# Three v buffers, an earlier unit 4, w1 in halves and earlier conversions in an attention and expert kernel on one core

## The chip, the cores and the metric

The kernel runs on one core of a Trainium2 chip. The metric is the device time of one execution in microseconds (us). A change of about 2% is what can be told from no change with this kernel. "Profile" means one execution recorded by the hardware profiler; its span is the part in which the core works, and the execution's own time is a little longer.

## The reference

```python
# q, k, v: (8 batches, 8 heads, 576, 64), fp32
scores = (q @ k.T) / sqrt(64)            # masked: 0 <= row - column < 64
attn = softmax(scores)
x = (attn @ v), heads side by side       # (8, 576, 512)
pooled = x.mean(axis=1)                  # (8, 512)
logits = pooled @ w_gate                 # (8, 8 experts)
e = argmax(logits); g = max(softmax(logits))
out[b] = g[b] * (relu(x[b] @ w1[e[b]]) @ w2[e[b]])   # w1: 512x1024, w2: 1024x512
```

Which expert's weights a batch needs is known only when its whole attention output has been pooled, so the load of w1 and w2 of a batch waits for its gate.

## The kernel before

The work is cut into 16 units `u`, each four heads of one batch; units 2b and 2b+1 are batch b. For a unit, q and k come in by `load_qk` as two tiles `qn` and `kn` (the transfer turns fp32 into bf16), TensorE transposes them (`transpose_qk`), and `leave_qk` copies them out of PSUM: q on ScalarE (ACT), k on VectorE (DVE) unless told otherwise. `scores(u, c)` makes a third of the banded scores and their exponentials; from unit 2 on DVE multiplies them with a mask. `values(u, s)` multiplies with v and `norm` divides by the row sums into `x`. `transpose_x` turns x round and sums it for the gate.

v of a batch is loaded once by `load_v(b)`: a memset of one element on GpSimd (POOL) claims the buffer `vn`, then SyncE (SP) issues the transfer. `cast_part` turns half a batch, one unit, into two fp16 copies: "whole" makes `va`, and "low" and "high" make `vb`, the same rows shifted by 64. `cast_v` does all three on DVE.

`gate(b)` ends with a register load on GpSimd; `load_w1` and `load_w2` then issue the weights (fp32 to fp16) from GpSimd's queue. Batch 0's w1 comes in four column quarters. An expert is eight `expert_up` and five `expert_down` chunks; `experts(amount)` emits the next chunks between the pieces of attention, so the experts of batch b run beside the attention of later units. Output rows leave through six `ob` buffers, copied by DVE and issued by SyncE. `busy(n)` emits n matmuls that nothing uses.

The order of everything on each engine is the order in which it is written: first a prelude that ends with units 0 to 3 and the first gate, then a loop over steps t = 4 to 19, in which unit t's attention, the preparation of unit t+1 and the expert chunks alternate. In even steps `next_gate` runs the gate of batch t/2 - 1 and issues its weights. GpSimd issues q, k and weights on one queue (q0 in the profile), SyncE v and the output on another (q1).

Of the kernel before, what the change touches and what calls it, by code (L numbers as in the profile page):

```python
# [156 lines left out]
def kernel(  # L157
# [22 lines left out]
    def P(ins):  # L180
        tc.keep_in_program_order(ins)
        return ins

    const = ctx.enter_context(tc.tile_pool(name="const", bufs=1))
    qkn = ctx.enter_context(tc.tile_pool(name="qkn", bufs=6))
    vpool = ctx.enter_context(tc.tile_pool(name="vpool", bufs=2))
    qkt = ctx.enter_context(tc.tile_pool(name="qkt", bufs=2))
    ptp = ctx.enter_context(tc.tile_pool(name="ptp", bufs=6))
    xpool = ctx.enter_context(tc.tile_pool(name="xpool", bufs=2))
# [18 lines left out]
    def load_qk(u):  # L208
        qn = qkn.tile([128, 2, NT * D], BF16, tag="qn")
        kn = qkn.tile([128, 2, NT * D], BF16, tag="kn")  # L210
        P(nc.gpsimd.dma_start(out=qn, in_=qv[u]))
        P(nc.gpsimd.dma_start(out=kn, in_=kv[u]))
        qk_tiles[u] = (qn, kn)

    v_tiles = {}

    def load_v(b):
        vn = vpool.tile([128, NM, D], FP32, tag="vn")

        P(nc.gpsimd.memset(vn[:, 0, 0:1], 0.0))  # L220
        P(nc.sync.dma_start(out=vn, in_=vv[b]))
        v_tiles[b] = vn

# [13 lines left out]
    load_qk(0)  # L237
    ident = const.tile([128, 128], BF16)
    make_identity(nc, ident)
    load_v(0)  # L240
    load_qk(1)
    identh = const.tile([128, 128], FP16)
    P(nc.vector.tensor_copy(out=identh, in_=ident))
# [220 lines left out]
    w2q = moe_w2.rearrange("e (g p i) d -> e p g i d", p=128, i=2)  # L464

    gparts = {}

# [46 lines left out]

    experts_of = {}

    NQ = 4

    def w1_parts():
        return weights[0][0].rearrange("p k f -> p (k f)").rearrange(  # L520
            "p (h k f) -> p h k f", h=NQ, k=KB)

# [10 lines left out]
                in_=w1e[experts_of[b]].squeeze(0)))  # L533

    def load_w2(b):
        i = FB // NQ if b == 0 else 4
        P(nc.gpsimd.dma_start(
            out=weights[b][1].rearrange("p (g i) d -> p g i d", i=i),
            in_=(w2q if b == 0 else w2e)[experts_of[b]].squeeze(0)))

    h_tiles = {}

    def expert_up(b, ft):
        if b == 0:
            w1t, cols = w1_parts()[:, ft // 2], slice(ft % 2, 256, 2)
        else:
            w1t, cols = weights[b][0], slice(512 * (ft // 4) + ft % 4, 512 * (ft // 4 + 1), 4)
        xT = xt_tiles[b]
        if ft == 0:
            h_tiles[b] = hpool.tile([128, FB, S], FP16, tag="hT", name=f"hT{b}")  # L550
        hT = h_tiles[b]
        php = psum.tile([128, 2, 512], FP32, tag="ps")
        for kb in range(KB):
            for sc in range(2):
                P(nc.tensor.matmul(  # L555
                    out=php[:, sc, 0:288], lhsT=w1t[:, kb, cols],
                    rhs=xT[:, kb, ts(sc, 288)],
                    start=(kb == 0), stop=(kb == KB - 1)))
# [79 lines left out]
    def busy(n):  # L638

        sp = psum.tile([128, 2, 512], FP32, tag="ps", name="idle")  # L640
        for _ in range(n):
            P(nc.tensor.matmul(out=sp[:, 0, :], lhsT=spin[:, 0:128], rhs=spin,
                               start=True, stop=True))
# [33 lines left out]
    add_outside(0, 1)  # L677
    add_outside(0, 2)

    after = const.tile([128, 1], BF16)  # L680
    P(nc.gpsimd.tensor_copy(out=after, in_=kt_tiles[0][:, 0:1]))
    load_qk(2)
    load_qk(3)
    load_v(1)
    for c in range(3):
        scores(0, c)
    make_masks()
    transpose_qk(1, 0)
    transpose_qk(1, 1)
    cast_v(0)  # L690
    cast_part(1, "high", nc.gpsimd)
    cast_part(1, "low", nc.gpsimd)
    cast_part(1, "whole")
    for c in range(3):
        add_outside(1, c)
    for c in range(3):
        scores(1, c)
    busy(2)
    values(0, 0)
    values(0, 1)  # L700
    transpose_qk(2, 0)
    values(1, 0)
    values(1, 1)
    transpose_qk(2, 1, leave=False)
    leave_qk(2, 1, A)
    busy(2)
    pool_mm(0)
    busy(3)
    pool_mm(1)
    pool_parts()  # L710
    busy(2)
    gate(0, False)
    load_w1(0)
    cast_v(2)
    load_qk(4)
    load_v(2)
    load_w2(0)
    load_qk(5)
    load_qk(6)
    for c in range(3):  # L720
        scores(2, c)
        if c == 0:
            gate_weight(0)
    transpose_x(0, eng=A, parts=False)
    transpose_x(1, eng=V, parts=False)
    transpose_qk(3, 0)
    transpose_qk(3, 1)
    cast_v(3)
    busy(4)
    for c in range(3):  # L730
        scores(3, c)

# [12 lines left out]
    transpose_qk(4, 1)  # L745
    experts(1.0)
    transpose_x(3)
    load_v(3)

    for t in range(START + 1, NU + LAG):  # L750
        pace = per_step / 8.0 * 0.96
        on, prev, ahead = t < NU, START + 1 < t <= NU, t + 1 < NU

        def next_gate():
            b = t // 2 - 1
            gate(b)
            load_w1(b)
            if START + 1 < t < NU - 4:
                load_qk(t + 4)
            load_w2(b)  # L760
            if t == START + 1:
                load_qk(7)

        if t % 2 == 1 and (t + 3) // 2 < B:
            load_v((t + 3) // 2)
        for u in [8, 9] if t == 5 else [t + 4] if t % 2 == 1 else []:
            if u < NU:
                load_qk(u)
        if prev:
            transpose_x(t - 1)  # L770
        if t == NU:
            okc = row_check()
        if on:
            scores(t, 0)
        experts(pace)
        if t == START + 1:
            next_gate()
            cast_v(4)
        if on:
            scores(t, 1)  # L780
        experts(pace)
        if START + 1 < t <= NU and t % 2 == 0:
            next_gate()
        if on:
            scores(t, 2)
        experts(pace)
        if ahead:
            transpose_qk(t + 1, 0)
            cast_part(t + 1, "whole")
        experts(pace)  # L790
        if on:
            values(t, 0)
        if ahead:
            cast_part(t + 1, "low")
        experts(pace)
        if ahead:
# [48 lines left out]
```

## Time and profile before

| what | value |
|---|---|
| median of 3 runs | 237.91 us (236.73 to 240.49) |
| profiled execution | 237.41 us, span 235.7 us, mean granted clock 0.973 |
| PE / DVE / ACT / POOL busy | 207.7 / 142.3 / 121.5 / 42.8 us |
| first gate's w1 issued, first expert matmul | 28.71, 33.43 us |
| q0 / q1 moved | 26.22 / 18.88 MB |

PE is TensorE, PEld its weight loads. A row of the timeline gives the start and length in us, engine, line and operation, the tiles written and read, the number of instructions, and in brackets how long the engine sat idle before it and what ended that. A row of the chain gives start, length and what the end of the program hung on then. In the tables by stretch the clock that TensorE was granted and the share of the 16 DMA engines stand behind the engines; that share is a sum over overlapping packets and can pass 1.

### The profile page before, as it was taken

How to read it: one execution, taken by the hardware profiler on the slowest of the kernel's cores; microseconds unless marked ns; L12 is line 12 of the kernel's file. 1: busy time of each engine (PE TensorE's matmuls, PEld its weight loads, DVE VectorE, ACT ScalarE, POOL GpSimd, SP SyncE). 2: the span in 40 equal slices, each digit the busy share in tenths (PEclk: the TensorE clock that was granted, in tenths of full speed). 3: DMA queues.
4: the chain of work that ended last, by engine and by line, in shares of the span. 5: the costliest groups of instructions: out<-in, count | busy, mean ns of one | idle time of the engine just before them, and what ended most of it. 6: DMA issues, size and time to landing. Idle time of an engine off the chain costs nothing.

```text
span 235.7 us, 7000 instructions
## 1 busy us (share of the span) xinstructions
PE 207.7 (88%) x3020; PEld 141.4 (60%) x3020; DVE 142.3 (60%) x315; ACT 121.5 (52%) x205; POOL 42.8 (18%) x72
## 2 busy tenths in 40 slices
PE   7657879979799978999899989999999999998980
PEld 2427557725478545875578556865687558647640
DVE  2559597539856594838764697559675964531140
ACT  2461576933376606693467617680758265605500
POOL 7252192041300160007000330020001100200000
PEclk9995899979999999999999999999999999999997
DMA  5999299999999999997999999999960995199342
GB/s 76 221 216 256 47 116 220 236 243 246 228 247 265 246 243 250 230 247 152 228 244 235 198 180 261 229 253 173 246 177 3 161 233 169 11 197 237 116 145 66
DMA packets 31222, 45.64 MB, mean 194 GB/s; under 512 B 2512, under 2 KB 22992, under 8 KB 31184
## 3 DMA queue, kind: packets, MB, share of 16 engines
q0 software_dynamic: 15152, 26.22, 63.2%
q1 hardware_dynamic: 15232, 18.88, 26.7%
q8 instruction: 25, 0.41, 0.7%
q10 hardware_dynamic: 800, 0.03, 0.2%
q14 instruction: 13, 0.11, 0.1%
HBM read 61.90 MB, written 9.44 MB: 303 GB/s over the span
## 4 chain that ended last, share of the span: by engine, by line
PE 46%; DMA 24%; ACT 11%; DVE 11%; issue 3%; POOL 1%; POOLq 1%; SPq 0%
PE php L555 23%; DMA w1t<-in_moe_w_dram 19%; PE pso L569 9%; DMA vn<-in_v_dram 5%; PE tp L329 5%; PE op L408 4%; ACT xT L453 4%; ACT pt L384 4%; ACT hT L559 3%; DVE vb L298 2%; DVE dst L298 2%; DVE pt L386 2%; PE tp L445 2%; DVE ob L572 1%; PE sp L369 1%
## 5 line engine op out<-in xcount | busy, mean ns | idle before, releaser
L555 PE MATMUL php<-xT,w1t 128*128 128x288 f16 x512 | 71.5, 288 | 5.3 <-DMA w1t<-in_moe_w_dram 4.7
L559 ACT ACTIVATE hT<-php,gatew 128x576 f16<-128x576 f32 x64 | 47.4, 746 | 33.3 <-PE php L555 33.3
L569 PE MATMUL pso<-w2t,hT 128*128 128x512 f16 x256 | 61.6, 386 | 2.6 <-DMA w2t<-in_moe_w_dram 1.8
L555 PEld LDWEIGHTS <-w1t 128*128 128x128 f16 x512 | 53.6, 113 | 13.3 <-DMA w1t<-in_moe_w_dram 5.6
L384 ACT ACTIVATE pt<-sp 128x768 f16<-128x768 f32 x48 | 37.7, 813 | 13.8 <-PE sp L369 13.8
L569 PEld LDWEIGHTS <-hT 128*128 128x128 f16 x256 | 23.4, 99 | 29.2 <-issue 3.0
L453 ACT ACTIVATE xT<-tp 128x576 f16<-128x576 f16 x28 | 17.9, 646 | 33.5 <-PE tp L445 33.5
L572 DVE COPY ob<-pso 128x512 f32<-128x512 f32 x32 | 21.9, 685 | 19.9 <-PE pso L569 19.6
L386 DVE TENSOR_TENSOR pt<-pt,masks 128x768 f16<-128x768 f16 x42 | 23.1, 557 | 17.3 <-ACT pt L384 16.8
L531 POOL DMA_DIRECT2D w1t<-in_moe_w_dram x7 | 5.0, 717 | 139.0 <-DVE gatew L513 75.1
L424 DVE TENSOR_TENSOR x<-op,linv 128x640 f16<-128x640 f32 x32 | 26.4, 824 | 1.1
L342 ACT COPY dst<-tp 128x1152 bf16<-128x1152 bf16 x16 | 18.0, 1124 | 12.1 <-PE tp L329 12.1
L298 DVE COPY dst<-tp 128x1152 bf16<-128x1152 bf16 x15 | 20.3, 1350 | 4.3 <-PE tp L329 4.0
L408 PE MATMUL op<-vb,pt 128*64 128x65 f16 x320 | 17.7, 202 | 4.1 <-DVE vb L298 3.5
L408 PEld LDWEIGHTS <-pt 128*64 128x64 f16 x640 | 14.4, 116 | 10.7 <-issue 6.0
L408 PE MATMUL op<-va,pt 128*64 128x65 f16 x320 | 17.4, 202 | 0.0
L369 PE MATMUL sp<-dst 64*64 64x128 bf16 (+1 forms) x672 | 15.4, 214 | 1.9 <-DVE dst L298 1.9
L298 DVE CAST va<-vn 128x1152 f16<-128x1152 f32 x16 | 12.7, 796 | 5.9 <-DMA vn<-in_v_dram 5.8
L298 DVE COPY vb<-va 64x1152 f16<-64x1152 f16 (+1 forms) x30 | 15.8, 527 | 0.6
L369 PEld LDWEIGHTS <-dst 64*64 64x64 bf16 x672 | 10.4, 106 | 8.9 <-issue 4.4
L476 DVE SCALAR_TENSOR_TENSOR gpart<-wg,pooled,gpart 128x8 f32<-128x8 f32 x21 | 4.8, 226 | 17.9 <-ACT xT L453 17.9
L445 PE MATMUL tp<-identh,x 128*128 128x128 f16 x160 | 11.6, 220 | 3.3 <-DVE x L424 2.5
(69 smaller groups left out, 166.6 us busy)
## 6 DMA issues: line engine op xcount, KB each, us to landing
w2t<-in_moe_w_dram POOLq DMA_DIRECT2D x8, 1024.0 KB, 17.5
out_dram<-ob SPq DMA_DIRECT2D x32, 256.0 KB, 8.6
w1t<-in_moe_w_dram POOLq DMA_DIRECT2D x7, 1024.0 KB, 10.2
qn<-in_q_dram POOLq DMA_DIRECT2D x16, 288.0 KB, 15.3
kn<-in_k_dram POOLq DMA_DIRECT2D x16, 288.0 KB, 16.5
w1t<-in_moe_w_dram POOLq DMA_DIRECT2D x4, 256.0 KB, 6.1
out_dram<-ob SPq DMA_DIRECT2D x16, 64.0 KB, 6.5
vn<-in_v_dram SPq DMA_DIRECT2D x8, 0.2 KB, 18.1
```

The costliest lines, as they stand in the source:

```text
L298: P(eng.tensor_copy(out=out, in_=in_))
L342: P(nc.scalar.copy(out=dst.rearrange("p (x r t) -> p x r t", x=2, t=NT), in_=view))
L369: P(nc.tensor.matmul(out=sp[64 * half:64 * half + 64, s, 64 * (qblk - 6 * c):64 * (qblk - 6 * c) + n], lhsT=kT[64 * s:64 * s + 64, ts(kblk ...
L384: P(nc.scalar.activation(out=pt, in_=sp[:, :, 0:384], func=AF.Exp, scale=scale))
L386: P(nc.vector.tensor_tensor(out=pt, in0=pt, in1=masks[:, c].rearrange("p s g w -> p s (g w)"), op=ALU.mult))
L408: P(nc.tensor.matmul(out=op[64 * half:64 * half + 64, xx, 65 * jj:65 * jj + 65], lhsT=pt[:, s, 64 * (g % 6):64 * (g % 6) + 64], rhs=win, s ...
L424: P(nc.vector.tensor_tensor(out=x[:, :, h0 * D:(h0 + 2) * D].rearrange("p j (x c) -> p x j c", x=2), in0=view[:, :, :, 0:64], in1=li[:, :, ...
L453: P(nc.scalar.activation(out=xT[:, kb, :], in_=tp[:, kl, 0:S], func=AF.Copy, accum_out=pooled[:, b, kb:kb + 1]))
L555: P(nc.tensor.matmul(out=php[:, sc, 0:288], lhsT=w1t[:, kb, cols], rhs=xT[:, kb, ts(sc, 288)], start=(kb == 0), stop=(kb == KB - 1)))
L559: P(nc.scalar.activation(out=hT[:, ft].rearrange("p (sc s) -> p sc s", sc=2), in_=php[:, :, 0:288], func=AF.Relu, scale=gatew[:, b:b + 1]))
L569: P(nc.tensor.matmul(out=pso[:, 0, :], lhsT=hT[:, fb, ts(mt, 128)], rhs=w2t[:, fb, :], start=(fb == 0), stop=(fb == FB - 1)))
L572: P(nc.vector.tensor_copy(out=ob, in_=pso[:, 0, :]))
```

## The change

Prelude: v of batch 0 is issued between q and k of unit 0; v of batch 1 is claimed by a copy from k of unit 0; GpSimd converts vb of unit 0 and DVE does all of unit 1, where GpSimd had unit 1; units 3 and 4 are loaded behind these conversions, unit 4 thus ahead of the first gate; w1 of batch 0 comes in halves, w2 right behind it in the layout of the other batches; v of batch 2 is claimed by a copy from the first half of w1; four `busy` calls are shorter or gone; k of unit 3 leaves on ScalarE; units 2 and 3 are converted later. Loop: `load_v` moves from the head of odd steps into `next_gate`, for a batch that is two steps further on, into a third buffer; conversions of unit t+1 stand in the first half of step t from t = 6 on.

```diff
-    vpool = ctx.enter_context(tc.tile_pool(name="vpool", bufs=2))
+    vpool = ctx.enter_context(tc.tile_pool(name="vpool", bufs=3))
...
         P(nc.gpsimd.dma_start(out=qn, in_=qv[u]))
+        if u == 0:
+            load_v(0)
         P(nc.gpsimd.dma_start(out=kn, in_=kv[u]))
...
-    def load_v(b):
+    def load_v(b, behind=None):
         vn = vpool.tile([128, NM, D], FP32, tag="vn")
-        P(nc.gpsimd.memset(vn[:, 0, 0:1], 0.0))
+        if behind is None:
+            P(nc.gpsimd.memset(vn[:, 0, 0:1], 0.0))
+        else:
+            P(nc.gpsimd.tensor_copy(out=vn[:, 0, 0:1], in_=behind))
...
-    NQ = 4
+    NQ = 2
...
-    after = const.tile([128, 1], BF16)
-    P(nc.gpsimd.tensor_copy(out=after, in_=kt_tiles[0][:, 0:1]))
+    load_v(1, kt_tiles[0][:, 0:1])
     load_qk(2)
-    load_qk(3)
-    load_v(1)
...
-    cast_v(0)
-    cast_part(1, "high", nc.gpsimd)
-    cast_part(1, "low", nc.gpsimd)
-    cast_part(1, "whole")
+    cast_part(0, "high", nc.gpsimd)
+    cast_part(0, "low", nc.gpsimd)
+    load_qk(3)
+    load_qk(4)
+    cast_part(0, "whole")
+    cast_v(1)
...
-    busy(2)
     values(0, 0)
     values(0, 1)
     transpose_qk(2, 0)
+    busy(1)
     values(1, 0)
     values(1, 1)
+    pool_mm(0)
     transpose_qk(2, 1, leave=False)
     leave_qk(2, 1, A)
-    busy(2)
-    pool_mm(0)
-    busy(3)
+    busy(1)
     pool_mm(1)
     pool_parts()
-    busy(2)
     gate(0, False)
     load_w1(0)
-    cast_v(2)
-    load_qk(4)
-    load_v(2)
     load_w2(0)
     load_qk(5)
+    load_v(2, w1_parts()[:, 0, 0, 0:1])
     load_qk(6)
+    load_v(3)
...
-    transpose_qk(3, 1)
+    transpose_qk(3, 1, leave=False)
+    leave_qk(3, 1, A)
+    cast_v(2)
     cast_v(3)
-    busy(4)
+    busy(3)
...
             load_w2(b)
+            if t // 2 + 2 < B:
+                load_v(t // 2 + 2)
...
-        if t % 2 == 1 and (t + 3) // 2 < B:
-            load_v((t + 3) // 2)
...
+        if ahead and t > 5:
+            cast_part(t + 1, "whole")
         if on:
             scores(t, 0)
...
             next_gate()
-            cast_v(4)
+        if ahead and t > 5:
+            cast_part(t + 1, "low")
         if on:
             scores(t, 1)
...
+        if ahead and t > 5:
+            cast_part(t + 1, "high")
...
         if on:
             scores(t, 2)
+        if t == START + 1:
+            cast_v(t)
         experts(pace)
         if ahead:
             transpose_qk(t + 1, 0)
-            cast_part(t + 1, "whole")
...
-        if ahead:
-            cast_part(t + 1, "low")
...
         if on:
             values(t, 1)
-        if ahead:
-            cast_part(t + 1, "high")
+        if t in (4, 5):
+            cast_v(t + 1)
```

Lines from 205 on have other numbers in the changed kernel (the copy of line 298 is 303 there, the transfer of v in line 221 is 227).

First place: GpSimd from the first v to the first gate. `vn` is v as loaded, `vb_122` a shifted fp16 copy, `eidx` the expert's number. Before:

```order
L212 DMA kn<-in_k_dram 128x2x576
L211 DMA qn<-in_q_dram 128x2x576
L212 DMA kn<-in_k_dram 128x2x576
L220 MEMSET vn 128x1
L298 COPY vb_122<-vn 64x18x64 x2
L501 TENSOR_LOAD eidx
L528 ISA
L528 DMA w1t_579<-in_moe_w_dram 128x4x256
```

And in the changed kernel:

```order
L226 COPY vn<-dst 128x1
L211 DMA qn<-in_q_dram 128x2x576
L214 DMA kn<-in_k_dram 128x2x576
L303 COPY vb_122<-vn 64x17x64
L303 COPY vb_122<-vn 64x18x64
L211 DMA qn<-in_q_dram 128x2x576
L214 DMA kn<-in_k_dram 128x2x576
L211 DMA qn<-in_q_dram 128x2x576
L214 DMA kn<-in_k_dram 128x2x576
L505 TENSOR_LOAD eidx
L532 ISA
L532 DMA w1t_572<-in_moe_w_dram 128x4x512
```

Two more units of q and k stand between the conversions and the gate; the claim of the second v went ahead of unit 2.

Second place: SyncE's queue, v (`vn`) against the writes of the output (`out_dram`). Before:

```order
L221 DMA vn<-in_v_dram 128x36x64 x4
L573 DMA out_dram<-ob 128x512 x3
L586 DMA out_dram<-ob 64x256 x2
L573 DMA out_dram<-ob 128x512
L221 DMA vn<-in_v_dram 128x36x64
L573 DMA out_dram<-ob 128x512 x3
L586 DMA out_dram<-ob 64x256 x2
L221 DMA vn<-in_v_dram 128x36x64
```

And in the changed kernel:

```order
L227 DMA vn<-in_v_dram 128x36x64 x5
L576 DMA out_dram<-ob 128x512 x3
L589 DMA out_dram<-ob 64x256 x2
L576 DMA out_dram<-ob 128x512 x2
L227 DMA vn<-in_v_dram 128x36x64
L576 DMA out_dram<-ob 128x512 x2
L589 DMA out_dram<-ob 64x256 x2
```

The fifth v moved ahead of all writes of batch 0, and the sixth ahead of all but one of batch 1's.

Third place: DVE in step 6, around the gate (`gmx`, `graw`) of batch 2; `pt` are the exponentials being masked, `va` and `vb` the conversions, `ob` an output tile. Before:

```order
L386 TENSOR_TENSOR pt<-pt,masks 128x768 x2
L572 COPY ob<-pso 128x512
L488 MAX gmx<-gl 128x8
L490 MAX_INDEX graw<-gmx,gl 128x8
L491 TENSOR_SCALAR eidx<-graw 128x8
L494 TENSOR_SCALAR gnm<-gmx 128x1
L513 RECIPROCAL gatew<-gsum 128x1
L386 TENSOR_TENSOR pt<-pt,masks 128x768
L298 COPY va_121<-vn 128x18x64
```

And in the changed kernel:

```order
L303 COPY va_121<-vn 128x18x64
L391 TENSOR_TENSOR pt<-pt,masks 128x768
L303 COPY vb_123<-va_121 64x18x64
L391 TENSOR_TENSOR pt<-pt,masks 128x768
L303 COPY vb_123<-va_121 64x18x64
L575 COPY ob<-pso 128x512
L492 MAX gmx<-gl 128x8
```

The three conversions moved from behind the gate to ahead of it, one before each mask and one between the second mask and the gate.

More of the change, by code (lines that the diff above doesn't have):

```diff
@@ L239 @@
     make_identity(nc, ident)
-    load_v(0)
     load_qk(1)
@@ L463 @@
     w2e = moe_w2.rearrange("e (g p i) d -> e p g i d", p=128, i=4)
-    w2q = moe_w2.rearrange("e (g p i) d -> e p g i d", p=128, i=2)
     gparts = {}
@@ L535, in load_w2 @@
     def load_w2(b):
-        i = FB // NQ if b == 0 else 4
         P(nc.gpsimd.dma_start(
-            out=weights[b][1].rearrange("p (g i) d -> p g i d", i=i),
-            in_=(w2q if b == 0 else w2e)[experts_of[b]].squeeze(0)))
+            out=weights[b][1].rearrange("p (g i) d -> p g i d", i=4),
+            in_=w2e[experts_of[b]].squeeze(0)))
     h_tiles = {}
@@ L544, in expert_up @@
         if b == 0:
-            w1t, cols = w1_parts()[:, ft // 2], slice(ft % 2, 256, 2)
+            w1t, cols = w1_parts()[:, ft // 4], slice(ft % 4, 512, 4)
         else:
@@ L747 @@
     transpose_x(3)
-    load_v(3)
     for t in range(START + 1, NU + LAG):
```

## The prediction

> **What bounds the kernel now.** I read the table of TensorE's waits first, then the chain that ended last, then the places in the timeline where the two meet. TensorE is busy for 207.7 of 235.7 us, so time can only go where it waits, where its clock is low, or before its expert matmuls begin. Its longest waits (total us, times, longest):
>
> ```profile
> PE php L555 <- DMA w1t<-in_moe_w_dram: 4.7, 4, 1.7
> PE op L408 <- DVE vb L298: 3.5, 2, 2.4
> PE tp L445 <- DVE x L424: 2.5, 3, 1.5
> ...
> PE pso L569 <- DMA w2t<-in_moe_w_dram: 1.8, 1, 1.8
> ```
>
> No wait is large; they fall into the start and the first batches. The chain of waits through the start (start us, us, what):
>
> ```profile
> 2.22 0.72 POOL kn L212
> ...
> 3.66 12.18 DMA vn<-in_v_dram
> 15.86 0.77 DVE va L298
> ...
> 17.97 1.29 DVE vb L298
> 19.30 1.25 PE op L408 x38
> ...
> 21.52 1.10 PE op L408 x40
> ...
> 23.58 0.96 PE idle L642 x2
> ...
> 24.79 0.85 PE idle L642 x3
> ```
>
> The reader is to see that the first v is the long pole: it is issued at 3.66 and lands at 15.86, its conversions end at 19.26, and then TensorE runs its work in a row to the gate, 1.81 us of it idle matmuls. The table by stretch (PE, weight load, DVE, ACT, POOL busy; granted clock, DMA share, GB/s) shows a clock near half for that row of work, and DMA engines that are empty just behind it:
>
> ```profile
> 18.00:25.00 7.00, 5.91 (x129) 4.85 (x130) 6.00 (x10) 2.24 (x2) 0.94 (x1) 0.52 1.07 237
> 25.00:27.00 2.00, 1.94 (x41) 1.15 (x43) 0.56 (x3) 0.00 (x0) 0.00 (x0) 0.99 0.07 16
> ```
>
> From the timeline, TensorE where the experts begin and where they first starve:
>
> ```profile
> 32.79 0.71 PE L369 MATMUL sp<-dst 64*64 64x64 bf16 x42 [1.00 <-DVE dst L298]
> 33.43 2.13 PE L555 MATMUL php<-xT,w1t 128*128 128x288 f16 x16
> ...
> 49.45 3.31 PE L569 MATMUL pso<-w2t,hT 128*128 128x512 f16 x8 [1.77 <-DMA w2t<-in_moe_w_dram]
> ...
> 56.34 1.90 PE L569 MATMUL pso<-w2t,hT 128*128 128x512 f16 x8
> ...
> 64.78 1.17 PE L555 MATMUL php<-xT,w1t 128*128 128x288 f16 x8 [1.68 <-DMA w1t<-in_moe_w_dram]
> ```
>
> The wait for the first w2 costs twice: 1.77 us, and then eight matmuls that take 3.31 us where the same eight take 1.90 later, 1.41 us of lost clock.
>
> **The change part by part. First v (a gain of 0.8).** Its issue moves ahead of k of unit 0, from 3.66 to about 2.4 (k's own issue began at 2.22, and a memset goes ahead). That bounds the gain by 1.2 from above and by 0 from below, for it shares the engines with the same four q and k transfers. I take 0.8: v is the last of the five to end, so its early bytes count, but k of unit 0 comes later. Scores of unit 0 wait for that k; they have spare time until 19.30.
>
> **Conversions of unit 0 (a gain of 0.4).** GpSimd now makes unit 0's vb straight from the fp32 tile; DVE did it in two copies after va. GpSimd's two casts, then of unit 1, are the first row here:
>
> ```profile
> 15.96 2.97 POOL L298 CAST vb<-vn 64x1152 f16<-64x1152 f32 x2 [2.40 <-DMA vn<-in_v_dram]
> 28.71 3.00 POOL L528 DMA_DIRECT2D w1t<-in_moe_w_dram  x4 [9.78 <-DVE va L298]
> 30.56 1.17 ACT L342 COPY dst<-tp 128x1152 bf16<-128x1152 bf16 x1
> ```
>
> From landing to the end of vb it was 19.26 - 15.86 = 3.40; it becomes about 0.1 + 2.97. What is queued behind these casts on GpSimd is the issue of q and k of units 3 and 4, four of 0.72 us, done by about 21, well ahead of the gate.
>
> **Idle matmuls (a gain of 0.85).** 0.96 + 0.85 us of them leave the row; two single ones come in, at 0.48 each on that clock. The two ahead of the first values stood in a wait and are worth nothing. Normalising on DVE covers the rest: its last x is ready about when the second pooling begins, so no more than this can be had. Together the first gate and the issue of w1 move by 0.8 + 0.4 + 0.85 = 2.05, from 28.71 to 26.66.
>
> **w1 in halves (gives 0.75 of that back).** After the gate ScalarE, not DVE, now copies k of unit 3: behind the 30.56 row (end 31.73) another copy like it, 1.12 behind the first, ends at 32.85, where DVE's ended just ahead of the 32.79 row. So the scores of unit 3 and the first php would follow at 33.5 - 2.05 = 31.45. But the first half must have landed. Landing times of w1's transfers (us), and the rate of the quarters' packets (queue: packets, MB, share, in 31 to 36 us):
>
> ```profile
> DMA to landing us min/median/max: 3.9/8.7/14.8
> q0 software_dynamic: 1437, 0.71, 111.6%
> ```
>
> The fastest quarter (256 KB) landed after 3.9. The other 256 KB of a half cost 1.8 more at 0.71 MB in 5 us, about 1.3 at the 0.18 MB/us that 4 KB packets reach in the rows further below; halves have packets between these. I take 5.4 (5.2 to 5.7; 7.5 if unit 4's q and k are still ahead of it): landing 32.1, php 1.3 earlier than 33.43. Bounds for the whole start: 2.05 at best, a loss of 0.7 at worst.
>
> **w2 behind w1, unit 4 ahead of the gate (a gain of 3.2).** Unit 4's q and k, 288 KB each, now fill the stretch with a DMA share of 0.07. w2 follows w1 directly: half of w1 and w2 are 1.5 MB, some 8.5 us at 0.18, so w2 lands near 41 and is wanted at 49.45 - 1.77 - 1.3 = 46.4. The wait and its cold matmuls go: 1.77 + 1.41 = 3.18. Only if w2 came 5 us later would it return.
>
> **w1 of batch 1 (a gain of 1.7).** It took 14.79 where the next took 10.24 (chain of waits), because units 5 and 6 were still ahead in the queue; in the last two rows (queue: packets, MB, share in 58 to 64 us) it moves beside v:
>
> ```profile
> 49.95 14.79 DMA w1t<-in_moe_w_dram
> ...
> 81.76 10.24 DMA w1t<-in_moe_w_dram
> ```
> ```profile
> q0 software_dynamic: 286, 1.09, 89.6%
> q1 hardware_dynamic: 283, 0.29, 17.3%
> ```
>
> In 49 to 56 us, beside v as well, the rows of the same view were:
>
> ```profile
> q0 software_dynamic: 844, 0.92, 75.7%
> q1 hardware_dynamic: 788, 0.79, 40.4%
> ```
>
> With unit 4 and w2 out of the way the q and k of units 5 and 6, 1.2 MB at 0.92 MB in 7 us, follow the 41 of w2 and are through at 50; w1's 1.05 MB at 1.09 MB in 6 us, with some 1 around it, lands near 57, and TensorE wants it at 63.1 - 4.5 = 58.6. The wait of 1.68 goes, with 1.6 to spare. The third v waits for the first half of w1 at 32.1. Its 1.18 MB move at 0.29 MB in 6 us beside w2 to 41, then at 0.79 MB in 7 us beside units 5 and 6: it lands near 49 as an estimate. Unit 4's conversion, 1.9 on DVE behind a mask, ends near 52, and its values, which stand just ahead of the 56.34 row, want it near 51.6: a loss of 0.4 (0 to 2).
>
> **Early conversions (a loss of 0.4).** From step 6 the last of three conversions stands on DVE between the second mask and the gate. Chain rows of the gate of step 6, and timeline rows behind it:
>
> ```profile
> 78.96 0.56 DVE pt L386
> 79.52 0.60 DVE ob L572
> 80.24 0.26 DVE graw L490 x2
> ```
> ```profile
> 87.93 0.46 DVE L298 COPY vb<-va 64x1152 f16<-64x1152 f16 x1
> ...
> 87.96 0.73 PE L445 MATMUL tp<-identh,x 128*128 128x128 f16 x10 [1.51 <-DVE x L424]
> ...
> 92.05 1.17 PE L555 MATMUL php<-xT,w1t 128*128 128x288 f16 x8 [0.94 <-DMA w1t<-in_moe_w_dram]
> ...
> 118.24 1.17 PE L555 MATMUL php<-xT,w1t 128*128 128x288 f16 x8 [1.03 <-DMA w1t<-in_moe_w_dram]
> ```
>
> Mask, copy and gate follow each other without a gap, so 0.46 goes onto the gate and onto w1 behind it. It counts where TensorE waits for w1, in batches 2 and 3: 0.9. In return x is ready sooner; the 1.51 is followed by a wait for w1 and is lost there, of the other 1.0 (2.5 in the first table) I take 0.5. Bounds: 1.5 lost (0.46 at three more gates), 2.5 gained. Where the new v issue follows w2's, its packets alternate with w1's one by one (286 against 283 above), and w1 keeps 0.18 MB/us: nothing.
>
> **The sum:** 1.3 + 3.2 + 1.7 - 0.4 - 0.4 = 5.4. The profiled execution took 237.41 (span 235.7), 0.5 below the median of 237.91: 232.0.
>
> On the clock: 18 to 25 us ran at 0.52 after a pause of 2.4 and one of 1.1, and the w2 wait of 1.77 was enough for cold matmuls. [...] I stay with the rows and give that a fifth of the forecast's chance.
>
> **The rivals.** (1) *Writes stuck behind v, slower.* SyncE's queue now has the fifth v ahead of all writes of batch 0, and later each v ahead of four of a batch's five. Issue to landing (KB each, us; and v's min/median/max):
>
> ```profile
> out_dram<-ob SPq DMA_DIRECT2D x32, 256.0 KB, 8.6
> ```
> ```profile
> DMA to landing us min/median/max: 12.2/18.1/30.8
> ```
>
> A write behind a median v lands after 18.1 + 8.6 = 27; behind one that takes 30.8, after 39. Six buffers hold the five tiles of a batch and one more, so a buffer is wanted again about one batch on, 27 us (64.78 to 92.05). With the long v DVE stalls for 12 at its copies in batch 1, and TensorE with it: 232.0 + 12 = 244. It decides once a write takes over 27. For it: two v (the fourth and fifth) now stand in a row there. Against: the first table has no wait for a write, and these v are issued before the first writes are ready. (2) *The transfers are the bound.* From batch 1 to 2 the DMA share is above 1 throughout:
>
> ```profile
> 64.78:92.00 27.22, 24.53 (x370) 16.95 (x370) 17.85 (x38) 15.63 (x27) 4.39 (x7) 1.00 1.11 250
> ```
>
> Then all that an earlier start wins is waited for at w1 of batches 2 and 3, save the empty stretch of about 2 us: 235.4. Against: these waits were only 0.94 and 1.03. (3) *The half of w1 lands late*, at 7.5 for 5.4, behind unit 4, and the clock falls in that wait: 2.1 + 1.4 back, 235.5.
>
> **How the numbers follow.** The forecast has 0.50 (its own range 229 to 234.5), the transfers 0.19, the late half 0.17, the writes 0.14. Over 2% is under 233.15 or above 242.7, about what a measurement of this kernel can tell from no change. Faster: 0.42 of the forecast's 0.50, and 0.07 from the tails of (2) and (3), 0.49. Slower: 0.10 of the writes' 0.14, and 0.02 unnamed, 0.12. The rest, 0.39, is within. From below the range takes the best start (0.75) and the full gain in x (2.0): 229.2; from above it takes in both middle cases and a mild form of the writes: 239.5.
>
> **What would show it.** v converts near 15; values begin near 18.1; w1 is issued near 26.7; php begins near 32.1; no wait of pso for w2, its first eight matmuls take 1.9; no wait at w1 of batch 1; w1's later landings stay near 10.5. Wrong: a DVE copy to ob that waits for a write, a first php after 33.4, or waits for w1 of over 2 us in batches 2 to 4.

## The result, and the profile after

The changed kernel takes 234.57 us (median of 4 runs, 233.94 to 234.69) against 237.64 (236.73 to 240.49) for the kernel before on the same chip: a ratio of 0.988, 95% interval 0.984 to 0.992. That is a real gain of 1.2%, but under the 2% from which the forecast calls a kernel faster. The time forecast was 232.0: the gain is 2.7 us in the profiled spans (235.7 to 233.0) where 5.4 were worked out. All ratios here are of undisturbed executions; one profile below, that of "quarters", comes from an execution of 238.63 us, 1.7% above that kernel's median.

TensorE's longest waits in the changed kernel, in the columns of the first table (total us, times, longest):

```profile
PE php L558 <- DMA w1t<-in_moe_w_dram: 2.2, 3, 1.2
PE tp L334 <- DMA kn<-in_k_dram: 2.1, 2, 1.6
PE op L413 <- DVE pt L391: 1.4, 2, 0.8
```

The wait for w2 is gone, that for w1 is half of its 4.7. New are a longer wait for k, at the start, and one for a mask's product (`pt`). The timeline of TensorE at the rows that the prediction used, where each batch's expert begins:

```profile
33.06 2.15 PE L558 MATMUL php<-xT,w1t 128*128 128x288 f16 x16
...
47.33 1.90 PE L572 MATMUL pso<-w2t,hT 128*128 128x512 f16 x8
...
61.62 1.17 PE L558 MATMUL php<-xT,w1t 128*128 128x288 f16 x8 [0.86 <-DMA w1t<-in_moe_w_dram]
...
87.68 1.17 PE L558 MATMUL php<-xT,w1t 128*128 128x288 f16 x8 [0.17 <-DMA w1t<-in_moe_w_dram]
...
209.77 2.52 PE L558 MATMUL php<-xT,w1t 128*128 128x288 f16 x19 [1.20 <-DMA w1t<-in_moe_w_dram]
```

and the last of these rows in the kernel before:

```profile
213.10 3.13 PE L555 MATMUL php<-xT,w1t 128*128 128x288 f16 x24 [1.03 <-DMA w1t<-in_moe_w_dram]
```

From such rows comes a table of where the 2.7 us arose (start of a batch's first php; batch 3 begins at 118.24 before and 113.38 after):

| stretch | before | after | gain | forecast |
|---|---|---|---|---|
| to php of batch 0 | 33.43 | 33.06 | 0.37 | 1.3 |
| to the end of its first eight pso matmuls | 19.33 | 16.17 | 3.16 | 3.2 |
| to php of batch 1 | 12.02 | 12.39 | -0.37 | 1.3 (1.7 - 0.4) |
| batch 1 to batch 3 | 53.46 | 51.76 | 1.70 | -0.4, |
| batch 3 to batch 7 | 94.86 | 96.39 | -1.53 | for all |
| batch 7 to the end of the span | 22.60 | 23.23 | -0.63 | the rest |

### The profile page after: what moved, and what is told of

It is laid out like the page before. It is cut to its first block, busy times and chain, and to the rows that moved or that the text cites. A ratio compares the mean times of both kernels' runs of the same rounds, so it can differ in the third digit from the quotient of the medians.

```text
span 233.0 us, 6978 instructions
## 1 busy us (share of the span) xinstructions
PE 205.6 (88%) x3012; PEld 142.2 (61%) x3012; DVE 140.1 (60%) x314; ACT 122.5 (53%) x206; POOL 41.2 (18%) x69
## 4 chain that ended last, share of the span: by engine, by line
PE 50%; DMA 17%; ACT 14%; DVE 13%; issue 3%; POOL 1%; POOLq 0%; ACTq 0%
PE php L558 22%; DMA w1t<-in_moe_w_dram 13%; PE pso L572 13%; ACT xT L458 4%; DMA kn<-in_k_dram 4%; ACT pt L389 4%; PE tp L334 4%; PE op L413 4%; ACT hT L562 3%; PE tp L450 3%; DVE x L429 2%; DVE pt L391 2%; PE sp L374 2%; PE pso L581 2%; DVE dst L303 2%
## 5 line engine op out<-in xcount | busy, mean ns | idle before, releaser
L572 PE MATMUL pso<-w2t,hT 128*128 128x512 f16 x256 | 60.2, 380 | 1.9 <-DVE ob L575 0.8
L558 PEld LDWEIGHTS <-w1t 128*128 128x128 f16 x512 | 54.6, 115 | 10.4 <-DMA w1t<-in_moe_w_dram 3.0
L391 DVE TENSOR_TENSOR pt<-pt,masks 128x768 f16<-128x768 f16 x42 | 23.3, 555 | 9.8 <-ACT pt L389 9.1
L303 DVE COPY dst<-tp 128x1152 bf16<-128x1152 bf16 x14 | 19.0, 1356 | 8.7 <-PE tp L334 8.6
L413 PE MATMUL op<-vb,pt 128*64 128x65 f16 x320 | 16.8, 196 | 4.5 <-DVE pt L391 1.4
L413 PEld LDWEIGHTS <-pt 128*64 128x64 f16 x640 | 13.5, 110 | 11.0 <-issue 6.2
L374 PE MATMUL sp<-dst 64*64 64x128 bf16 (+1 forms) x672 | 16.0, 219 | 2.8 <-DVE dst L303 1.1
L413 PE MATMUL op<-va,pt 128*64 128x65 f16 x320 | 16.5, 197 | 0.0
L303 DVE COPY vb<-va 64x1152 f16<-64x1152 f16 (+1 forms) x30 | 13.9, 464 | 0.6
L450 PE MATMUL tp<-identh,x 128*128 128x128 f16 x160 | 12.6, 231 | 1.5 <-DVE x L429 1.1
L450 PEld LDWEIGHTS <-x 128*128 128x128 f16 x160 | 10.7, 104 | 4.2 <-DVE x L429 2.9
```

The costliest lines, as they stand in the source:

```text
L303: P(eng.tensor_copy(out=out, in_=in_))
L374: P(nc.tensor.matmul(out=sp[64 * half:64 * half + 64, s, 64 * (qblk - 6 * c):64 * (qblk - 6 * c) + n], lhsT=kT[64 * s:64 * s + 64, ts(kblk ...
L391: P(nc.vector.tensor_tensor(out=pt, in0=pt, in1=masks[:, c].rearrange("p s g w -> p s (g w)"), op=ALU.mult))
L413: P(nc.tensor.matmul(out=op[64 * half:64 * half + 64, xx, 65 * jj:65 * jj + 65], lhsT=pt[:, s, 64 * (g % 6):64 * (g % 6) + 64], rhs=win, s ...
L450: P(nc.tensor.transpose(out=tp[:, kl, ts(jj, 128)], in_=x[:, jj, x_chunk(b, kb)], identity=identh))
L558: P(nc.tensor.matmul(out=php[:, sc, 0:288], lhsT=w1t[:, kb, cols], rhs=xT[:, kb, ts(sc, 288)], start=(kb == 0), stop=(kb == KB - 1)))
```

## The experiments

Each edit is to the changed kernel unless its heading says otherwise. The ratios are to the kernel before, run beside it on the same chip; the changed kernel's is 0.988 (0.984 to 0.992). The table puts beside them the starts of php in each run's profile, read as above.

| kernel | ratio (95%) | php of batch 0, 1, 2, 3, 7 | span |
|---|---|---|---|
| the change | 0.988 (0.984-0.992) | 33.06, 61.62, 87.68, 113.38, 209.77 | 233.0 |
| high behind the gate | 0.983 (0.980-0.987) | 32.93, 61.59, 88.58, 113.68, 208.20 | 230.9 |
| late conversions | 0.984 (0.979-0.989) | 32.45, 61.05, 87.32, 112.41, 207.37 | 230.2 |
| v at odd steps | 0.999 (0.996-1.002) | 33.95, 63.00, 90.08, 115.87, 212.19 | 235.1 |
| first v behind k | 0.995 (0.992-0.998) | 34.09, 62.77, 88.64, 114.33, 210.48 | 233.5 |
| unit 4 behind w1 | 1.001 (0.997-1.005) | 33.20, 64.61, 90.39, 116.09, 212.29 | 234.8 |
| quarters | 0.994 (0.991-0.996) | 35.45, 64.64, 91.96, 117.66, 213.82 | 236.8 |
| before, with halves | 0.994 (0.991-0.997) | 34.17, 63.98, 90.49, 115.58, 210.26 | 233.3 |
| high behind the gate, va on ScalarE | 0.978 (0.976-0.980) | 33.10, 61.84, 87.73, 112.81, 207.25 | 229.9 |
| the last, fourth v behind w2 | 0.989 (0.985-0.993) | 33.27, 61.22, 88.82, 114.32, 208.85 | 231.5 |
| the last but one, unit 6 behind w1 | 0.986 (0.981-0.992) | 33.67, 62.15, 88.59, 113.69, 208.24 | 231.5 |

The first start varies by 1.5 us between profiles with the same code ahead of it (32.45 to 33.95 in the first four rows), so differences of that size there say nothing. From batch 1 on the differences repeat closely: batch 3 to 7 took 96.2 to 96.4 in the five kernels with the early high cast, and 94.4 to 95.0 in the seven without it, the kernel before among them.

### High behind the gate

```diff
-        if ahead and t > 5:
-            cast_part(t + 1, "high")
         experts(pace)
         if START + 1 < t <= NU and t % 2 == 0:
             next_gate()
+        if ahead and t > 5:
+            cast_part(t + 1, "high")
```

> The changed kernel with one move undone in effect: from step 6 on the third conversion ("high") stands behind the gate instead of ahead of it. Theory: it delays each gate of steps 6 to 14 by about 0.46, which is what the chain of the changed kernel shows between the mask and the gate from step 8 on; batches 3 to 6 then lose 1.5 in the changed kernel, and here that comes back: 1.0 to 1.5 faster than the changed kernel, 233.1 to 233.6. Rival: the gate hangs on ScalarE's exponentials anyway and the place of the conversion is worth nothing: 234.2 to 234.9.

The chain of waits at the gate of step 8 in the changed kernel shows the conversion between mask and gate (start us, us, what):

```profile
100.75 0.56 DVE pt L391
...
101.34 0.46 DVE vb L303
...
102.57 0.36 ACT gex L515 x2
102.93 0.71 ACT pt L389
...
103.67 0.57 DVE pt L391
...
104.28 0.31 PE op L413 x7
```

and TensorE's row there:

```profile
104.28 0.22 PE L413 MATMUL op<-vb,pt 128*64 128x65 f16 x1 [0.78 <-DVE pt L391]
```

With the cast behind the gate, the same two places:

```profile
101.66 0.56 DVE pt L391
102.22 0.10 DVE gmx L492
```
```profile
104.58 0.22 PE L413 MATMUL op<-vb,pt 128*64 128x65 f16 x1 [0.18 <-DVE pt L391]
```

From the mask to TensorE's row it is 3.53 us in the changed kernel and 2.92 after the edit, and the wait shrinks from 0.78 to 0.18. The delay does not reach TensorE through w1. It goes through ScalarE: the gate's exponential (`gex`) stands ahead of the third chunk of exponentials in ScalarE's order, and both wait for VectorE's gate work. Batches 3 to 7, with the three gates of steps 10, 12 and 14 that have a cast ahead of them, take 94.52 in place of 96.39: 0.62 per gate, just what the two rows differ by (0.61) and somewhat more than the cast itself. Batch 2 to 3, behind the gate of step 8, shrinks likewise, from 25.70 to 25.10. The theory holds in place and in sign, and the size is 0.6 for 0.46.

At the gate of step 6 the same cast reaches TensorE another way, through the `ob` copy that follows it on VectorE. The changed kernel and this one:

```profile
77.61 1.89 PE L572 MATMUL pso<-w2t,hT 128*128 128x512 f16 x8 [0.80 <-DVE ob L575]
```
```profile
78.55 1.89 PE L572 MATMUL pso<-w2t,hT 128*128 128x512 f16 x8 [0.21 <-DVE ob L575]
```

The ratios, 0.983 and 0.988, point the same way, but their intervals overlap. In this profile batch 1 to 2 takes 26.99 for 26.06 all the same: behind its wait of 0.98 for w1 the first two php chunks ran on a lower clock (0.61 from 64 to 66 us) and took 1.65 and 2.08 for the usual 1.17.

### Late conversions

From step 6 on, all three parts stand again where the kernel before has them:

```diff
-        if ahead and t > 5:
-            cast_part(t + 1, "whole")
...
             transpose_qk(t + 1, 0)
+            if t > 5:
+                cast_part(t + 1, "whole")
...
             values(t, 0)
+        if ahead and t > 5:
+            cast_part(t + 1, "low")
...
             values(t, 1)
+        if ahead and t > 5:
+            cast_part(t + 1, "high")
```

> The changed kernel with the conversions of the later steps (from step 6 on) back where they were: va behind the transposes of q, low behind the first values, high behind the second values. Theory, from the run with high behind the gate (ratio 0.983 against the changed kernel's 0.988): the early places cost the gates 0.45 each, and bring less than that elsewhere; then this kernel is faster than the changed one, ratio 0.980 to 0.986, and no 0.4 to 0.8 wait for a mask's product or for the gate's exponential is left from step 8 on. Rival, the purpose of the early places: x comes later again (the transposes of x wait 1 to 1.5 for VectorE at batches 2 to 7), 2 us in all; then the ratio is 0.990 to 0.997.

0.984: as fast, within the intervals, as with high alone moved. Batches 3 to 7 take 94.96, as before (94.86). What the early places of "whole" and "low" bring is thus 0.44 over three gates, where the early "high" costs 1.87. The wait of 1.51 for x returns in batch 1 (0.48 in the changed kernel), the gate of step 6 loses its cast, and batch 1 to 2 takes 26.27 for 26.06.

### v at odd steps

```diff
-            if t // 2 + 2 < B:
-                load_v(t // 2 + 2)
...
+        if t % 2 == 1 and (t + 3) // 2 < B:
+            load_v((t + 3) // 2)
```

> The changed kernel with the loads of v in the loop back at the head of odd steps (three buffers and all else as changed). In the changed kernel w1 of batch 1 was issued at 49.27, but its queue stood empty from 50.7 to 54.2, until SyncE's blocked issue of the fifth v ended at 53.60 and a stretch of DVE copies at 53.61. Theory S: the blocked issue of the fifth v holds w1's start; without it w1 lands about 8.5 to 9.5 after its issue instead of 12.3, and the wait of 0.86 at batch 1 goes: about 0.5 to 1 faster than the changed kernel. [...] Theory W (the rival named before: writes behind v): the writes of batch 0 land earlier, but nothing waited for them, so nothing changes by that.

1.1% slower than the change by the ratios. In the profile, w1 of batch 1 is no earlier (its first 4-KB packet again came 5.0 us after its issue), so the theory that SyncE's blocked issue of the fifth v holds it up falls. What the odd steps cost stands one batch on: batch 1 to 2 takes 27.08 for 26.06, with this wait at its end:

```profile
90.08 1.17 PE L558 MATMUL php<-xT,w1t 128*128 128x288 f16 x8 [1.20 <-DMA w1t<-in_moe_w_dram]
```

The changed kernel waits 0.17 there. So in this kernel the new place of v's issue behind w2, which the prediction priced at nothing, takes 1.0 off the wait for w1 of batch 2. It is not the only way there: the kernel before with halves (below) has v at odd steps too and waits 0.19.

### First v behind k

```diff
-        if u == 0:
-            load_v(0)
...
     make_identity(nc, ident)
+    load_v(0)
```

> The changed kernel with the first v back behind k of unit 0 and the identity, as before the change. Theory: issuing v first is worth nothing, because k of unit 1 lands 2.3 later by it (14.5 against 12.2) and its copy on DVE pushes back the conversions of v: the first normalising on DVE stays at 20.0 plus or minus 0.5, the first php at 33.1 plus or minus 0.4, the time within 0.4 of 234.6. The prediction's reading: v lands later by 0.5 to 0.8, and everything behind it too; php near 33.7, about 235.2.

0.7% slower than the change by the ratios (the intervals just miss each other), so the early v is worth something, about 1.6 us. This profile's first php is at 34.09, hardly outside what one and the same start shows by chance, so the profiles do not size it.

### Unit 4 behind w1, quarters, and halves alone

Three runs took the prediction's largest term apart. First, unit 4's q and k between w1 and w2 again, halves kept:

```diff
     load_qk(3)
-    load_qk(4)
...
     load_w1(0)
+    load_qk(4)
     load_w2(0)
```

> The changed kernel with q and k of unit 4 loaded again between w1 and w2 of batch 0 instead of ahead of the gate. Theory: the early unit 4 is what took away the wait for w2; here w2 lands 4 to 5 later (near 44 to 45 instead of 40), which is still ahead of 47.3, so the layout and the order of w2 alone suffice and the wait stays away, but w1 of batch 1 loses: 0 to 1 slower. Rival (the full 3.2 of the prediction hangs on unit 4): the wait for w2 of over 1.5 and the slow eight matmuls return, 237 to 238.

It is 1.4% slower than the change by the ratios. Its first pso has no wait and takes 1.90 for eight matmuls, but then the third v is late, and unit 4's conversion and values with it (rows of TensorE):

```profile
47.47 1.90 PE L572 MATMUL pso<-w2t,hT 128*128 128x512 f16 x8
...
54.24 0.22 PE L413 MATMUL op<-vb,pt 128*64 128x65 f16 x1 [2.12 <-DVE vb L303]
```
Second, w1 of batch 0 in quarters and w2 in 2-KB pieces again, unit 4 kept early:

```diff
-    NQ = 2
+    NQ = 4
...
-            out=weights[b][1].rearrange("p (g i) d -> p g i d", i=4),
-            in_=w2e[experts_of[b]].squeeze(0)))
+            out=weights[b][1].rearrange("p (g i) d -> p g i d", i=i),
+            in_=(w2q if b == 0 else w2e)[experts_of[b]].squeeze(0)))
```

> The changed kernel with w1 of batch 0 in four quarters and w2 of batch 0 in 2-KB pieces, as before; unit 4's loads stay ahead of the gate. Theory A: the wait for w2 ahead of the first second-layer matmul comes back, at 0.7 to 1.8 us, with cold matmuls behind it; the first php starts up to 0.75 earlier; all in all 1 to 2.5 us slower than the changed kernel: ratio 0.992 to 0.998. Theory B: the early unit 4 alone takes the w2 wait away; then it is as fast as the changed kernel or 0.5 faster: ratio 0.985 to 0.988.

Third, the kernel before with the reverse of this edit (`NQ = 2` and `w2e` throughout), nothing else:

> The kernel before with w1 of batch 0 in two halves instead of four quarters and w2 of batch 0 in 4-KB pieces, nothing else. Theory A, from the run with unit 4 moved back (there w2 was on time without unit 4's early loads): the size of the pieces alone takes away the wait of 1.77 for w2 and the cold matmuls behind it, and costs up to 0.75 for the half that lands later: 1.8 to 2.6 us faster than before at batch 0, of which the late third v takes back some at batch 1: ratio 0.989 to 0.997. Theory B, the prediction's step: unit 4's q and k ahead of w1 are needed for it; then the w2 wait stays at 1 us or more, and the ratio is 0.998 to 1.004.

The first pso of the one and of the other, with no wait ahead of it:

```profile
49.64 1.90 PE L574 MATMUL pso<-w2t,hT 128*128 128x512 f16 x8
```
```profile
49.98 1.90 PE L568 MATMUL pso<-w2t,hT 128*128 128x512 f16 x8
```

Either part alone takes the wait for w2 away. In the kernel before, halves cost something at the start, where php now waits for the first half, and bring 0.6% in all:

```profile
34.17 3.45 PE L554 MATMUL php<-xT,w1t 128*128 128x288 f16 x16 [1.65 <-DMA w1t<-in_moe_w_dram]
```

In the changed kernel quarters are 0.6% slower by the ratios, but the intervals (0.991 to 0.996 and 0.984 to 0.992) overlap by a hair, and its profile has a start 2 us late; whether halves are needed beside the early unit 4 stays open. What the early unit 4 brings beyond w2 is clear from the first of the three: without it the values of unit 4 wait 2.12, with it 0.30.

### What holds up w1 of batch 1

In the changed kernel w1 of batch 1 is issued at 49.27 and lands 12.30 later, where the next takes 8.39. The chain of waits, and the packets of 50.9 to 54.2 us (queue: packets, MB, share):

```profile
49.27 12.30 DMA w1t<-in_moe_w_dram
...
79.24 8.39 DMA w1t<-in_moe_w_dram
```
```profile
q1 hardware_dynamic: 708, 0.72, 111.6%
```

There is no row for q0: w1's queue moves nothing for 3.3 us while the fourth v, on q1, has the 16 DMA engines to itself. The first 4-KB packet comes 5.0 us after the issue, at the later batches 1.4. (Until 50.7 its queue still moved q and k of unit 6.) I first blamed VectorE, which runs without a gap just then (49.44 to 54.59): if its copies held w1 up, the delay would shrink at batch 1 with fewer of them and grow at step 8 with more. The test leaves out the conversion of unit 4 (batch 2 then uses an old v) and puts eight copies behind the gate of step 8:

```diff
-        if t == START + 1:
-            cast_v(t)
...
+        if t == 8:
+            for _ in range(8):
+                P(nc.vector.tensor_copy(out=spare, in_=masks[:, 0:2]))
```

> The changed kernel without the conversion of unit 4's v in step 4 (batch 2's output is then computed with an old v), and with eight extra SBUF-to-SBUF copies on VectorE right behind the gate of step 8. The time is no result; the trace is read at the two gates, for the delay from the issue of w1 to its first 4-KB packet: 5.0 us at batch 1 and 1.45 to 1.6 us at the later ones in the changed kernel. [...] Rival: the queue or the transfers under way (the third v) set it; then it stays near 5 at batch 1 and at 1.5 at step 8.

The rival holds. At batch 1 the delay is still 5.0. At step 8, VectorE's copies and the issue of w1 (rows of VectorE and of GpSimd), and q0 in 107.2 to 110.2 us:

```profile
105.22 5.27 DVE L792 COPY spare<-masks 128x1536 f16<-128x1536 f16 x8
```
```profile
105.72 0.78 POOL L535 DMA_DIRECT2D w1t<-in_moe_w_dram  x1 [20.17 <-PE tp L334]
```
```profile
q0 software_dynamic: 110, 0.45, 102.1%
```

1.5 us after the issue w1 moves, in the middle of the copies: these eight did not hold it up.

Two more runs changed what stands in the queues, both on top of the best kernel (next heading). In one the fourth v is issued behind w2 of batch 1:

```diff
     load_qk(6)
-    load_v(3)
...
             load_w2(b)
+            if t == START + 1:
+                load_v(3)
```

> The kernel with high behind the gate and va of unit 0 on ScalarE (0.978), and besides the fourth v issued behind w2 of batch 1, not ahead of the loop, so that only the third v is under way when w1 of batch 1 is issued near 49. It looks for what holds up w1 of batch 1 for 5 us although its queue is empty. Theory: the v's packets, which hold the transfer engines alone from 50.7 to 54; without the fourth v the first 4-KB packet comes 1.5 to 2.5 us after the issue, w1 lands near 58.5, before it is wanted at 60.8, and the wait of 1.04 at batch 1 goes: 0.5 to 1.0 us faster, ratio 0.974 to 0.976. Rival: the delay belongs to this issue itself (its place behind the loads issued before), and stays at 5; then the time stays (0.978) or rises, if the conversion of unit 6 then waits for the fourth v.

With no v under way w1's first packet comes 1.4 after the issue and php of batch 1 no longer waits for w1. But the kernel is 1.1% slower, because this v now lands late:

```profile
72.01 0.76 DVE L303 CAST va<-vn 128x1152 f16<-128x1152 f32 x1 [1.69 <-DMA vn<-in_v_dram]
```
```profile
85.73 0.73 PE L450 MATMUL tp<-identh,x 128*128 128x128 f16 x10 [1.79 <-DVE x L429]
```

In the other, unit 6's q and k move behind w1 of batch 1, so that the fourth v finishes earlier:

```diff
-    load_qk(6)
     load_v(3)
...
+            if t == START + 1:
+                load_qk(6)
             load_w2(b)
```

> The kernel with high behind the gate and va of unit 0 on ScalarE (0.978), and besides q and k of unit 6 loaded between w1 and w2 of batch 1 instead of ahead of the third batch's w1 wait, so that 0.6 MB less stands in the queues ahead of w1 of batch 1; the fourth v stays where it was. Theory one: w1 is held until the v ahead of it has left the engines. The v, which no longer shares with unit 6, ends 1.5 to 2.5 us earlier, near 51.5; w1's first 4-KB packet then comes 2 to 3 us after the issue, it lands near 59, and the wait of 1.04 at batch 1 goes: 0.5 to 1.0 us faster, ratio 0.973 to 0.976. Theory two: a start beside a busy second queue takes 4.6 to 5.2 us whatever that queue does; then the delay stays near 5, or w1 starts at 1.5 because the v had ended before. Rival for the time: unit 6's q, which is wanted at 64.3, now lands behind w1 near 61 to 66 and makes the transposes wait: 0.978 or worse.

Packets in 50 to 52 us:

```profile
q1 hardware_dynamic: 424, 0.43, 111.5%
```
Here v is alone until 52.0, w1's first packet comes at 52.04, 2.2 after the issue, and then w1 is alone. This fits theory one, that w1 starts when the v that has the engines is nearly through, early or late. In the changed kernel too, v's packets thin out near 54.5 and w1's begin at 54.28. But it is no rule: with unit 4 behind w1, the first packet of w1 comes at 53.7, 4.3 after its issue and right behind the last packets of its own queue, and the fourth v still has 0.5 MB or more of its 1.18 MB to go (q1 in 53.8 to 64.4 us; SyncE's next issue on it is through only at 64.5):

```profile
q1 hardware_dynamic: 505, 0.52, 18.1%
```
In the rows of 58 to 64 us in the prediction the two queues moved side by side, 286 packets and 283. In the late cases that fit theory one, w1's queue had stood empty beside a v that moved alone; why it is not let in then, no run here settles.

The time did not follow: 0.8% slower than without this edit. The wait for w1 of batch 1 is gone, and at batch 2 there is one of 1.18 where there was one of 0.60 (php of batch 2 at 88.59).

### The best version: high behind the gate, va on ScalarE

```diff
-    cast_part(0, "whole")
+    cast_part(0, "whole", A)
     cast_v(1)
```

and high behind the gate, as above.

> The changed kernel with the high cast behind the gate (as in the first experiment, 0.5% faster than the changed kernel) and, besides, unit 0's va conversion moved from VectorE to ScalarE, so that the two conversions of 2.37 us that stood one behind the other on VectorE (16.50 to about 21) run side by side. Theory: VectorE's queue ahead of the first normalising is on the path; the first normalising then comes 0.5 to 1.0 us earlier than 20.0, and the median is 0.5 to 1.0 us below the first experiment's: ratio to the kernel before 0.979 to 0.982. Rival: the values wait for GpSimd's vb conversions or ScalarE's exponentials instead; then the ratio stays at 0.983.

231.05 us, 0.978: 2.2% faster than the kernel before and 1.0% faster than the change. Its reason is only half shown. The cast at the gate accounts for about 0.5% by the ratios of the first experiment. The start is not earlier in the profile: the first normalising comes at 20.27. VectorE has one va less ahead of it, but its copies for `vb` take 1.86 together in place of 1.11, and k of unit 1 reached it 0.6 later in this profile (chain rows):

```profile
18.35 1.27 DVE vb L303
...
20.27 0.23 DVE linv L427
```

The median is 0.5% below the first experiment's, but the intervals (0.976 to 0.980, 0.980 to 0.987) touch, so what moving va brings, if anything, stays open.

## Why the prediction was right and wrong

The sign was right and the gain about half of what was worked out. The measured 234.57 lies just above the forecast's own 229 to 234.5 and nearer to the 235.4 of rival (2) and the 235.5 of rival (3) than to 232.0, so the number alone speaks no less for them. Of the four steps only the one for w2 came through as told; that the rest behind batch 1 summed to nearly the forecast -0.4 is luck.

**The start, 1.3 forecast, 0.37 in the profiles.** The first points came as told: GpSimd converted v from 15.36 ("near 15"), the half of w1 landed 5.2 after its issue, and the values began near 18.1:

```profile
18.30 0.19 PE L413 MATMUL op<-vb,pt 128*64 128x65 f16 x1 [0.95 <-POOL vb L303]
```

The miss lies between. The chain of waits through the changed start:

```profile
4.22 10.22 DMA kn<-in_k_dram
...
15.22 1.36 DVE dst L303
16.58 2.29 DVE va L303 x2
...
18.90 0.45 DVE vb L303
...
19.36 0.64 DVE vb L303
...
20.04 0.23 DVE linv L427
```

The long pole is no longer v but k of unit 1, which now stands behind v and lands at 14.4 instead of 12.2, and then VectorE: it copies that k, makes both va, and makes unit 1's vb, which GpSimd made before. The two va (ns, min/median/max) took, before and after:

```profile
L298 DVE CAST va<-vn x2: 760/760/761, 15.9 to 19.3; 128x1152 f16<-128x1152 f32 x2
```
```profile
L303 DVE CAST va<-vn x2: 753/1228/1702, 16.5 to 17.2; 128x1152 f16<-128x1152 f32 x2
```

The first of each pair ran beside GpSimd's casts and took 0.76 or 0.75 all the same; what held up the second in the changed kernel is open. The first normalising starts at 20.04, as it did before:

```profile
20.05 0.22 DVE L422 RECIPROCAL linv<-op 128x10 f32<-128x10 f32 x1
```

In the five profiles with this start it lies at 19.71 to 21.26, in the two with the old one at 20.05 and 20.31. So the steps "First v" and "Conversions of unit 0", 0.8 and 0.4, do not show at the first `norm`: I followed v, k of unit 0 and GpSimd, and did not write down what queued on VectorE ahead of it. Against that stands the run with the first v behind k, whose ratio gives the early v about 1.6 us; so the sum of both steps failed in the profiles, and what the early v alone is worth stays open. w1 was issued at 27.54, 1.17 earlier instead of 2.05, all of it behind the first normalising: 7.50 from there to the issue for 8.66. The shorter idle rows (0.85) would account for most of that, but it is not shown: the kernel before with halves has all of them and took 7.41 (20.31 to 27.72), with a granted clock of 1.00 from 16 to 30 us where the profile of the kernel before shows 0.52 from 18 to 25 (two idle matmuls in that row took 0.60, before 1.03).

**The w2 wait, 3.2 forecast, 3.16.** Right in size: no wait, and 1.90 for the eight matmuls, at a granted clock of 1.00 where the 3.31 before ran at 0.56. The cause is wider than that step says. It credits unit 4 ahead of the gate and w2 directly behind w1, and the quarters show that these are enough. But the larger pieces, w1 in halves and w2 in 4-KB pieces, are enough as well, with unit 4 still between w1 and w2, as the run with unit 4 behind w1 and the halves alone show; the step gives them no part in it.

**w1 of batch 1, 1.3 net forecast, -0.37.** The step that failed is "lands near 57": I took w1 to share with v from its issue, and it got no packet for 5 us. It landed at 61.57, and 0.86 of the 1.68 stayed. The 0.4 for unit 4's values was fair (0.30 and 0.43 at its two halves); a wait of 0.65 for an `ob` copy came in. And the runs that freed w1 gained nothing in time, since the wait passed on to the fourth v or to w1 of batch 2. That fits rival (2), the transfers as the bound, which I gave 0.19, between batches 1 and 3 (DMA share 1.11 and 1.03 from batch 1 to 2 and from 2 to 3 in the changed kernel); no run tests it by moving fewer bytes.

**Early conversions, -0.4 forecast.** The sum over everything behind batch 1 is -0.46, near the figure, by two errors that cancel. The cast costs 0.6 per gate, not 0.46, and it does so through the `ob` copy at step 6 and ScalarE's order from step 8 on, not through w1 in batches 2 and 3 alone: batch 3 to 7 lost 1.53 by itself, which was the lower bound of the whole term. And batch 1 to 3 came out 1.70 shorter, w1 of batches 2 and 3 landing 8.39 and 8.83 after its issue in place of 10.24 and 10.61. With v back at odd steps 1.1 of that is lost (52.87 for 51.76), so the new place of v, which I had set at nothing, bears on it; but the kernel before with halves takes 51.60 with v at odd steps, so it is not the whole cause, and the rest stays open. The 0.63 at the end is within what the same code shows by chance: the other kernels took 22.5 to 23.3 from batch 7 to the end.

**The other rivals.** Writes stuck behind v did not happen: VectorE never waited for a write to leave an `ob` buffer, though SyncE issued its first write only at 53.64, behind the v ahead of it. The half of w1 was on time. On the clock: the granted clock was 0.52 from 23 to 30 us in this profile. With the same code at the start the slow stretch lay elsewhere: near 15 us six matmuls from `outside` took 2.08 with high behind the gate and 2.10 with the late conversions, where they took 1.15 here, and near 25 us the gate's two `gl` took 0.36 in both, where they took 0.56 here. What sets its place no run shows. The fifth of the forecast's chance was my estimate for a clock that stays up from the values to the gate. In this profile it did so to 22 us (1.00, then 0.71 and 0.50 by steps of 2 us); in the other two those matmuls ran at their short times to the gate, and first php came at 32.93 and 32.45 for 33.06, within what identical code at the start differs by.

## What to carry to other kernels

When work moves from one engine to another, write down the whole queue of the engine that receives it, up to the next instruction that somebody waits for; a term that follows the moved data alone misses what it now stands ahead of. A short instruction put ahead of a gate can delay what stands behind that gate on every engine that takes part in it: here a copy of 0.46 us on VectorE cost 0.6 per gate through ScalarE's exponentials, which stand in a fixed order. And where transfers fill the engines, as here from batch 1 to 2 (DMA share 1.11), look for the next wait before counting the gain of an earlier load: in both runs that freed w1 of batch 1 it came back within a batch.

## What the runs showed of the hardware

In the changed kernel w1 of batch 1 got its first packet 5.0 us after its issue, with its queue empty for the last 3.3 of them while a v on the other queue had the 16 DMA engines to itself. It began as that v ran out, here (54.28) and where the v ended 2 us earlier (52.04); with no v under way it began 1.4 after its issue. In the run with unit 4 behind w1 it began at 53.7 with 0.5 MB or more of the v still to come, so this is not a rule. Identical code at the start put first php anywhere from 32.45 to 33.95, so a term of half a microsecond there cannot be read from one profile. VectorE's conversion of 128x1152 elements took 0.75 and 1.70 in the changed kernel while GpSimd was converting too, the slower one only in part; its 16-bit copies of 64 partitions took 1.28 each in the kernel before, beside GpSimd's two casts, and 0.46 later. A wait of 0.98 on TensorE was followed by a granted clock of 0.61 in one profile (high behind the gate, php chunks of 1.65 and 2.08), and one of 1.02 at the same place in another (v at odd steps) by 1.00 (chunks of 1.17).
